# Convolution rows loaded two steps ahead, gathers placed through the step, and the second batch's convolution rearranged

## The chip, the cores and the metric

The kernel runs on one core of one Trainium2 chip. The metric is the device time of one execution in microseconds (us). The times given are the median of three runs and the profile of one further execution.

## The reference

For each of 8 batches of 4224 tokens with 192 channels the reference computes a causal convolution over 7 tokens, with one softmax-normalised set of taps for each of 8 heads of 24 channels. It then takes the real part of a two-dimensional Fourier transform over tokens and channels, adds the convolved input, normalises each token, and adds a two-layer MLP of width 768:

```python
w = softmax(weight)                                # (8, 7)
x = einsum('hk,bskhg->bshg', w, unfold(x_padded))  # causal convolution
u = x + real(fft(fft(x, axis=1), axis=2))
un = (u - mean(u)) / sqrt(var(u) + 1e-6)           # over the 192 channels
out = u + maximum(un @ w_ch1, 0) @ w_ch2
```

All matrices are used as a sum of a high and a low float16 part, so a product takes three matmuls.

## The kernel before, in words

A batch goes through these parts.

- **Convolution** (`load_windows`, L330, and `conv_unit`, L387 to L395). The tokens come in 6 chunks of 720 rows. SyncE (SP) loads a chunk as a tile `xt` of 576 KB; there are two buffers for it. TensorE (PE) multiplies it by a band matrix, three units a chunk, into PSUM tiles `pc`; ScalarE (ACT) copies these to `xa` and stores them to a scratch `sc` in DRAM (the store is issued from ACT's queue). A pass on ACT (L343) sums the squares of `xt`. For the first batch one of three copies is on VectorE (DVE, L393).
- **Fourier transform along the tokens.** SP loads `sc` back in another order as four pieces `xs` (L456, 768 to 864 KB each in four transfers, two buffers). ACT writes the high part `XH` (L472), DVE the low part `XL` (L473), in two halves a piece. Only then is the buffer free for the piece after next. `stage_a` (16 units, PE tile `pa`, L490) needs all four pieces and writes `yh` and `yl` (L498, L499). `stage_b` (8 units, `pb`, L516) writes `V` (L524, L525).
- **A step** is one of 9 tiles of a batch; eight hold 512 tokens, the last 128. `prep` makes `pq` on PE (L577), moves it to `u` on ACT (L594), adds on GpSimd (POOL) the convolved rows `xr` (L595), takes statistics on DVE (L601), works out `y` and `nm` in seven small POOL instructions (L614 to L621), normalises to `un` on ACT (L625) and splits to `hl` (ACT L635, POOL L638). `xr` is fetched by four indirect gathers a tile (`load_res`, L543), issued by POOL, into three buffers. A DMA transpose (SP, L648) turns `hl` into `kt`.
- **MLP.** Six hidden units a step (`ph` on PE, L677; `hh` on ACT, L681; `hlo` on DVE, L682) and four output units (`po`, L696 to L702; `u` on DVE, L708). `ph` has two PSUM buffers, so PE stops when ACT is two units behind. SP stores `u` (L716).

The order of the work is written in the main loop over 72 steps. In step n the MLP of tile n runs, the normalisation and transpose of tile n+2, and the sums of tile n+3. Beside these, `front` gives each batch its convolution and transform at steps counted from its own first tile (`rel`): chunk by chunk at -18 to -13, the loads of `xs` at -10 to -8, the splits at -9 to -7, `stage_a` at -7 to -5. So three batches are in work at once, and the pattern repeats every 9 steps. Each engine runs its instructions in the order that a scheduling pass makes of this. SP is one such queue: window loads, `xs` loads, transposes and stores stand in it one behind the other, and an instruction that waits holds up all behind it. A window load is moreover anchored behind the last transpose (`turn[0]`).

Ahead of the loop stand the first batch and, after its first two transposes, all six chunks of the second batch's convolution.

Of the kernel before, what the change touches and what calls it, by code (L numbers as in the profile page):

```python
# [11 lines left out]
F32 = mybir.dt.float32  # L12
I32 = mybir.dt.int32
U32 = mybir.dt.uint32
AF = mybir.ActivationFunctionType
ALU = mybir.AluOpType
# [3 lines left out]
B, S, D, HID = 8, 4224, 192, 768  # L20
# [3 lines left out]
NCH = NW // WC  # L24
# [27 lines left out]
Q0 = NPAIR  # L52
# [73 lines left out]
def kernel(  # L126
# [13 lines left out]
    nc = tc.nc  # L140
    PSUM = bass.MemoryType.PSUM
    cp = ctx.enter_context(tc.tile_pool(name="cp", bufs=1))
    sb = ctx.enter_context(tc.tile_pool(name="sb", bufs=2))
# [179 lines left out]
    def load_windows(bt, ch, tag="xt", bufs=2):  # L323

        b = bt.b
        n = D if b < NB0 else HP * GRP
        src = xw[b] if b < NB0 else xv[b - NB0]
        xt = sb.tile([WP, WC, D], F32, tag=tag, name=f"xt_{b}_{ch}", bufs=bufs)[:, :, :n]
        with tc.issue_after(turn[0]) if turn[0] else ExitStack():
            nc.sync.dma_start(xt, src[:, ch * WC : (ch + 1) * WC])  # L330
        bt.xt[ch] = xt
# [38 lines left out]
    def conv_unit(bt, ch, part, xa_slot=("xa", 2)):  # L370

        b = bt.b
        xt = bt.xt[ch]
        if part == 0:
            if ch == 0:
                scratch(bt)
            if b:
                squares(bt, xt)
            bt.xa[ch] = sb.tile(
                [WR, WC, D], F32, tag=xa_slot[0], name=f"xa_{b}_{ch}", bufs=xa_slot[1]  # L380
            )
        xa = bt.xa[ch]
        h0 = 3 * part
        n = min(3, xt.shape[2] // GRP - h0)
        pc = ps.tile([128, 3, WC, GRP], F32, tag="f", name=f"pc_{b}_{ch}_{h0}", bufs=4)
        for h in range(h0, h0 + n):
            nc.tensor.matmul(  # L387
                pc[:WR, h - h0], band[:, h, :WR], xt[:, :, h * GRP : (h + 1) * GRP],
                start=True, stop=True,
            )  # L390
        to = xa[:, :, h0 * GRP : (h0 + n) * GRP].rearrange("p w (h g) -> p h w g", g=GRP)
        if b == 0 and part == 1:
            nc.vector.tensor_copy(to, pc[:WR, :n])  # L393
        else:
            nc.scalar.activation(to, pc[:WR, :n], AF.Copy)  # L395
        if part == 2:
            cols = slice(0, xt.shape[2])
            bt.last_store = store_rows(bt, xa[:, :, cols], ch * WC * WR, cols)
            if b == 0:
                squares(bt, xt)  # L400
            del bt.xt[ch], bt.xa[ch]
# [26 lines left out]
    def scales(bt):  # L428
        bt.c = pow2_of_norm(bt.nrm, bt.nsq, 15, f"x{bt.b}")
        bt.g = sb.tile([128, 1], F32, tag="g", name=f"g_{bt.b}")  # L430
        nc.vector.reciprocal(bt.g, bt.c)
        nc.vector.tensor_scalar_mul(bt.g, bt.g, GSC)
# [8 lines left out]
    def load_x(bt, i):  # L441

        b = bt.b
        b0, b1 = PIECES[i]
        tag, bufs = (("yh", 1), ("yl", 1))[i - 2] if b == 0 and i > 1 else ("xs", 2)
        xs = sb.tile([NA, 9, D], F32, tag=tag, name=f"xs_{b}_{i}", bufs=bufs)
        for ch in range(NA // AC):

            first = 33 * AC * ch + 128 * b0 - (S if b0 >= WRAP[ch] else 0)
            src = bass.AP(  # L450
                bt.sc.tensor,
                bt.sc.offset + first * D,
                [[33 * D, AC], [128 * D, b1 - b0], [1, D]],
            )
            with tc.issue_after(turn[0]) if b == 1 else ExitStack():
                load = nc.sync.dma_start(xs[AC * ch : AC * (ch + 1), : b1 - b0], src)  # L456
        bt.xs[i] = xs
        return load.ins
# [76 lines left out]
        bt.V[it] = V  # L535


    def load_res(bt, it):
        b = bt.b
        xr = sb.tile([128, 4, D], F32, tag="xr", name=f"xr_{b}_{it}", bufs=3)  # L540
        sc = bt.sc
        def gather(g, col):
            nc.gpsimd.indirect_dma_start(  # L543
                xr[:, g], None, sc[:S],
                bass.IndirectOffsetOnAxis(ap=rows_sb[:, col : col + 1], axis=0),
            )

        for g in range(1 if it == Q0 else 4):
            gather(g, 0 if it == Q0 else 1 + 4 * it + g)
        bt.xr[it] = xr  # L550

    def prep(bt, it):
        b = bt.b
        xr = bt.xr.pop(it)
        ng = 1 if it == Q0 else 4
        pq = ps.tile([128, ND, 2, NC], F32, tag="f", name=f"pq_{b}_{it}", bufs=4)
        u = sb.tile([128, 4, D], F32, tag="u", name=f"u_{b}_{it}", bufs=5)
# [41 lines left out]
        mv = sb.tile([128, 4, 2], F32, tag="mv", name=f"mv_{b}_{it}", bufs=3)  # L599
# [8 lines left out]
        y = sb.tile([128, 4], F32, tag="y", name=f"y_{b}_{it}", bufs=3)[:, :ng]  # L608
        t = sb.tile([128, 4], F32, tag="t", name=f"t_{b}_{it}", bufs=3)[:, :ng]
        w = sb.tile([128, 4], F32, tag="w", name=f"w_{b}_{it}", bufs=3)[:, :ng]  # L610
        nm = sb.tile([128, 4], F32, tag="nm", name=f"nm_{b}_{it}", bufs=3)[:, :ng]
# [10 lines left out]
        yield  # L622
        un = sb.tile([128, 4, D], F32, tag="un", name=f"un_{b}_{it}", bufs=1)
        for g in range(ng):
            nc.scalar.activation(  # L625
                un[:, g], u[:, g], AF.Identity,
                bias=nm[:, g : g + 1], scale=y[:, g : g + 1],
            )
        yield


# [4 lines left out]
        for f, o in ((slice(0, 128), 256), (slice(128, D), D)):  # L636
            n = f.stop - f.start
# [105 lines left out]
    def call(f, *a):  # L743
        return lambda: f(*a)

    conv_at = {r: [r + 18] for r in range(-18, -12)}
    load_at = {-10: [0], -9: [1, 2], -8: [3]}
    split_at = {-9: [0, 1], -8: [2, 3, 4, 5], -7: [6, 7]}  # L750
    a_at = {-7: range(0, 4), -6: range(4, 10), -5: range(10, 16)}
    b_at = {-4: [0], -3: [1, 2], -2: [3], -1: [4], 0: [5, 6], 1: [7]}

    def front(bt, rel):
        units = []
        for ch in conv_at.get(rel, ()):
            if ch + 1 < NCH:
                units.append(call(load_windows, bt, ch + 1))
            units += [call(conv_unit, bt, ch, p) for p in range(3)]
        if rel == min(conv_at) - 1:  # L760
            units.append(call(load_windows, bt, 0))
        if bt.b > 1 and rel == max(conv_at) + 1:
            if bt.b >= NB0:
                units.append(call(conv_segments, bt))
            units.append(call(scales, bt))
        units += [call(load_x, bt, ch) for ch in load_at.get(rel, ())]
        units += [call(split_x, bt, i) for i in split_at.get(rel, ())]
        units += [call(stage_a, bt, t) for t in a_at.get(rel, ())]
        return units

    batches = [Batch(b) for b in range(B)]
# [51 lines left out]
    def sums(k):  # L823
        return [call(prep_piece, k)] * (2 if steps[k][1] == Q0 else 4)

    def rest(k):
        return [call(prep_piece, k)] * 2

# [7 lines left out]
        )  # L836
    with tc.issue_after(last_load):
        nc.sync.dma_start(rows_sb, rows)
        for ch in range(2):
            load_windows(batches[1], ch)  # L840
        for k in range(4):
            load_res(*steps[k])
    stage_b(first, 0)
    stage_b(first, 1)
    for f in sums(0) + sums(1) + rest(0):
# [2 lines left out]
    for f in rest(1):  # L848
        f()
    transposes(first, 1)  # L850
 
    for ch in range(NCH):
        for part in range(3):
            conv_unit(batches[1], ch, part)
        if ch + 2 < NCH:
            load_windows(batches[1], ch + 2)
    scales(batches[1])
    load_x(batches[1], 0)
    load_windows(batches[2], 0)
    stage_b(first, 2)  # L860
    for f in sums(2):
        f()
# [2 lines left out]
    for n in range(len(steps) + 1):  # L865
        bt, it = steps[n] if n < len(steps) else (None, 0)
        prev = steps[n - 1] if n else None
        if n + 4 < len(steps):
            load_res(*steps[n + 4])
        hid = [call(mlp_hidden, bt, it, hts) for hts in hidden_units(it)] if bt else []  # L870
        out = []
        if prev:
            out = [call(mlp_out, *prev, g) for g in range(1 if prev[1] == Q0 else 4)]
        main = []
        while hid or out:
            if hid:
                main.append(hid.pop(0))
            if out:
                main.append(out.pop(0))
        fill = []  # L880
        for f in batches:
            rel = n - f.b * NIT
            if n < len(steps) and (f.b or rel >= 0):
                fill += front(f, rel)
                fill += [call(stage_b, f, i) for i in b_at.get(rel, ())]

        at = {}

        def place(fs, first, step):
            for i, f in enumerate(fs):  # L890
                at.setdefault(min(first + i * step, len(main) - 1), []).append(f)

        if n + 2 < len(steps):
            place(rest(n + 2), 0, 1)
            place([call(transposes, *steps[n + 2])], 3, 1)
        if n + 3 < len(steps):
            place(sums(n + 3), 2, 2)
        merged = []
        for i, unit in enumerate(main):
            merged += [unit, *at.get(i, ())]  # L900
        spread(merged, fill)
# [58 lines left out]
```

## Time and profile before

| | |
|---|---|
| median of 3 runs | 1359.53 us (1359.05 to 1361.79) |
| profiled execution | 1354.9 us |
| its span, first to last instruction | 1353.0 us |
| PE busy in the span | 1193.2 us (88%) |
| ACT, DVE, POOL busy | 832.1, 738.0, 650.2 us |
| mean granted PE clock | 0.95 |

The span is the profiled execution without what lies around it (1.9 us here). A busy row of PE is time with a matmul in flight at the clock that was granted then, so a stretch at half clock counts double. A wait is the idle time of an engine ahead of an instruction, put down to what came last.

### The profile page before, as it was taken

How to read it: one execution, taken by the hardware profiler on the slowest of the kernel's cores; microseconds unless marked ns; L12 is line 12 of the kernel's file. 1: busy time of each engine (PE TensorE's matmuls, PEld its weight loads, DVE VectorE, ACT ScalarE, POOL GpSimd, SP SyncE). 2: the span in 40 equal slices, each digit the busy share in tenths (PEclk: the TensorE clock that was granted, in tenths of full speed). 3: DMA queues.
4: the chain of work that ended last, by engine and by line, in shares of the span. 5: the costliest groups of instructions: out<-in, count | busy, mean ns of one | idle time of the engine just before them, and what ended most of it. 6: DMA issues, size and time to landing. Idle time of an engine off the chain costs nothing.

```text
span 1353.0 us, 30083 instructions
## 1 busy us (share of the span) xinstructions
PE 1193.2 (88%) x12224; PEld 942.9 (70%) x12224; DVE 738.0 (55%) x1609; ACT 832.1 (62%) x1588; POOL 650.2 (48%) x1052
## 2 busy tenths in 40 slices
PE   4158679996999969999699969999889998999998
PEld 4145558785877848777587858878577775777766
DVE  7742635455655646456554555545675466555443
ACT  4655657557765757557665577656766567545642
POOL 0250455456445644447344562446654576456620
PEclk9588879998999979999799989999899999999999
DMA  8836466639554494636865376463944434223321
GB/s 269 208 99 183 120 153 174 124 98 163 147 123 108 107 183 114 129 101 106 181 144 129 104 126 166 121 124 89 213 113 111 123 89 95 71 63 86 74 62 39
DMA packets 225818, 170.18 MB, mean 126 GB/s; under 512 B 119560, under 2 KB 207440, under 8 KB 225680
## 3 DMA queue, kind: packets, MB, share of 16 engines
q1 hardware_dynamic: 163408, 108.53, 36.1%
q10 hardware_dynamic: 49600, 33.77, 9.7%
q0 software_dynamic: 12672, 25.97, 8.0%
q8 instruction: 95, 1.56, 0.5%
q14 instruction: 43, 0.35, 0.1%
HBM read 83.73 MB, written 58.55 MB: 105 GB/s over the span
## 4 chain that ended last, share of the span: by engine, by line
PE 42%; POOL 22%; issue 13%; DMA 9%; ACT 7%; DVE 5%; SPq 2%; ACTq 0%; POOLq 0%; DVEq 0%
PE ph L677 15%; POOL xr L543 10%; PE pa L490 5%; PE pc L387 5%; DMA xt<-in_xw_dram 5%; PE po L696 5%; PE po L702 4%; PE po L699 4%; POOL u L595 4%; POOL hl L638 3%; ACT un L625 2%; PE pq L577 2%; SPq L456 2%; ACT XH L472 1%; DVE XL L473 1%
## 5 line engine op out<-in xcount | busy, mean ns | idle before, releaser
L677 PE MATMUL ph<-kt,W 128*128 128x512 f16 (+1 forms) x2160 | 501.1, 365 | 44.2 <-DMA kt<-hl 29.8
L682 DVE SCALAR_TENSOR_TENSOR hlo<-ph,hh 128x512 f16<-128x512 f32 (+1 forms) x400 | 271.8, 681 | 395.2 <-ACT hh L681 394.7
L696 PE MATMUL po<-W,hh 128*128 128x192 f16 x1584 | 387.0, 247 | 7.3 <-ACT hh L681 6.3
L699 PE MATMUL po<-W,hh 128*128 128x192 f16 x1584 | 386.7, 247 | 0.0
L702 PE MATMUL po<-W,hlo 128*128 128x192 f16 x1584 | 384.1, 247 | 0.2 <-DVE hlo L682 0.2
L681 ACT ACTIVATE hh<-ph 128x512 f16<-128x512 f32 (+1 forms) x400 | 235.0, 590 | 214.8 <-PE ph L677 212.1
L543 POOL DMA_INDIRECT xr<-sc,rows_sb x264 | 276.3, 1046 | 133.3 <-issue 58.7
L677 PEld LDWEIGHTS <-W 128*128 128x128 f16 x2160 | 195.2, 99 | 190.4 <-issue 53.8
L638 POOL TENSOR_TENSOR hl<-un,hl 128x512 f16<-128x512 f32 (+1 forms) x144 | 127.8, 908 | 214.6 <-ACT hl L635 214.5
L595 POOL TENSOR_TENSOR u<-u,xr 128x768 f32<-128x768 f32 (+1 forms) x72 | 123.3, 1712 | 185.4 <-ACT u L594 185.4
L625 ACT ACTIVATE un<-u,nm,y 128x192 f32<-128x192 f32 x264 | 123.9, 537 | 86.6 <-POOL nm L621 84.4
L387 PE MATMUL pc<-xt,band 128*120 128x144 f32 x756 | 119.3, 308 | 65.4 <-DMA xt<-in_xw_dram 43.4
L696 PEld LDWEIGHTS <-hh 128*128 128x128 f16 x1584 | 155.1, 98 | 25.3 <-ACT hh L681 7.7
L702 PEld LDWEIGHTS <-hlo 128*128 128x128 f16 x1584 | 155.0, 98 | 19.7 <-issue 1.1
L699 PEld LDWEIGHTS <-hh 128*128 128x128 f16 x1584 | 155.3, 98 | 16.2 <-issue 1.3
L387 PEld LDWEIGHTS pc<-xt,band 128*120 128x120 f32 x756 | 111.0, 200 | 75.9 <-DMA xt<-in_xw_dram 45.3
L473 DVE SCALAR_TENSOR_TENSOR XL<-xs,s_x,XH 128x768 f16<-128x768 f32 x64 | 102.3, 1610 | 56.9 <-ACT XH L472 55.6
L472 ACT ACTIVATE XH<-xs,s_x 128x768 f16<-128x768 f32 x64 | 104.9, 1679 | 43.5 <-DMA xs<-sc 43.5
L490 PE MATMUL pa<-c_sb,XH 128*128 128x128 f16 x1024 | 104.8, 224 | 17.3 <-ACT XH L472 17.3
L499 DVE SCALAR_TENSOR_TENSOR yl<-pa,yh 99x512 f16<-99x512 f32 x128 | 86.4, 681 | 39.4 <-ACT yh L498 38.3
L708 DVE SCALAR_TENSOR_TENSOR u<-po,fo,u 128x384 f32<-128x384 f32 (+1 forms) x136 | 81.6, 600 | 37.4 <-PE po L702 36.7
L577 PE MATMUL pq<-c_sb,V 128*128 128x130 f16 (+1 forms) x1440 | 100.2, 215 | 1.2 <-DVE V L525 1.1
(124 smaller groups left out, 1424.3 us busy)
## 6 DMA issues: line engine op xcount, KB each, us to landing
out_dram<-u SPq DMA_DIRECT2D x64, 384.0 KB
xt<-in_xw_dram SPq DMA_DIRECT2D x42, 576.0 KB
sc<-xa ACTq DMA_DIRECT2D x42, 540.0 KB
xs<-sc SPq DMA_DIRECT2D x96, 192.0 KB
xs<-sc SPq DMA_DIRECT2D x32, 216.0 KB
xr<-sc,rows_sb POOLq DMA_INDIRECT x264
sc<-xa ACTq DMA_DIRECT2D x7, 450.0 KB
xt<-in_xv_dram SPq DMA_DIRECT2D x6, 504.0 KB
```

What stands on the lines that cost most here:

```text
L387: nc.tensor.matmul(pc[:WR, h - h0], band[:, h, :WR], xt[:, :, h * GRP : (h + 1) * GRP], start=True, stop=True,)
L490: nc.tensor.matmul(pa[:, i], x[:, at], F[:, l], start=(n == 0), stop=(n == 2))
L543: nc.gpsimd.indirect_dma_start(xr[:, g], None, sc[:S], bass.IndirectOffsetOnAxis(ap=rows_sb[:, col : col + 1], axis=0),)
L595: nc.gpsimd.tensor_tensor(u[:, :ng], u[:, :ng], xr[:, :ng], op=ALU.add)
L625: nc.scalar.activation(un[:, g], u[:, g], AF.Identity, bias=nm[:, g : g + 1], scale=y[:, g : g + 1],)
L638: nc.gpsimd.tensor_tensor(bl[:, :, o : o + n], un[:, :ng, f], hi[:, :, f], op=ALU.subtract)
L677: nc.tensor.matmul(ph[:, n], W1[:, w, ht * 128 : (ht + 1) * 128], kt[:, k], start=(i == 0), stop=(i == len(order) - 1),)
L681: anchor[0] = nc.scalar.activation(hh, ph, AF.Relu).ins
L682: nc.vector.scalar_tensor_tensor(hlo, ph, 0.0, hh, op0=ALU.max, op1=ALU.subtract)
L696: nc.tensor.matmul(po[:, g % 2], hh[:, ht, tk], W2[:, ht, 0], start=(ht == 0), stop=False)
L699: nc.tensor.matmul(po[:, g % 2], hh[:, ht, tk], W2[:, ht, 1], start=False, stop=False)
L702: nc.tensor.matmul(po[:, g % 2], hlo[:, ht, tk], W2[:, ht, 0], start=False, stop=(ht == 5),)
```

## The change

It has four parts.

1. For batches from the third on, a window load stands two chunks ahead of its convolution instead of one: chunks 0 and 1 are loaded in the two steps ahead of the first convolution, chunk c+2 behind the convolution of chunk c, whose buffer it takes. The convolutions move one step later (`rel` -17 to -12).
2. `load_res` issues one gather per call, and the calls are placed after units 1, 3, 5 and 7 of a step instead of together at its start.
3. The second batch's first four chunks are loaded at once into four tiles (two `xt` and two `xs` buffers) and convolved ahead of the loop; its last two chunks follow in step 0, its transform is loaded, split and run one or more steps later than before. All its convolution copies are on DVE.
4. The first two tiles are normalised on DVE instead of ACT.

```diff
-        if b == 0 and part == 1:
+        if b == 1 or b == 0 and part == 1:
             nc.vector.tensor_copy(to, pc[:WR, :n])
...
-    def load_res(bt, it):
+    def load_res(bt, it, g):
...
         for g in range(ng):
-            nc.scalar.activation(
-                un[:, g], u[:, g], AF.Identity,
-                bias=nm[:, g : g + 1], scale=y[:, g : g + 1],
-            )
+            if b == 0 and it < 2:
+                nc.vector.tensor_scalar(
+                    un[:, g], u[:, g], mv[:, g, 0:1], y[:, g : g + 1],
+                    op0=ALU.subtract, op1=ALU.mult,
+                )
+            else:
+                nc.scalar.activation(
+                    un[:, g], u[:, g], AF.Identity,
+                    bias=nm[:, g : g + 1], scale=y[:, g : g + 1],
+                )
...
-    conv_at = {r: [r + 18] for r in range(-18, -12)}
+    conv_at = {r: [r + 17] for r in range(-17, -11)}
...
+    conv_1 = {-9: [4, 5]}
+    load_1 = {-9: [0, 1], -8: [2, 3]}
+    split_1 = {-8: [0, 1], -7: [2, 3, 4, 5], -6: [6, 7]}
+    a_1 = {-6: range(0, 6), -5: range(6, 16)}
...
-        for ch in conv_at.get(rel, ()):
-            if ch + 1 < NCH:
-                units.append(call(load_windows, bt, ch + 1))
+        for ch in conv.get(rel, ()):
             units += [call(conv_unit, bt, ch, p) for p in range(3)]
-        if rel == min(conv_at) - 1:
-            units.append(call(load_windows, bt, 0))
-        if bt.b > 1 and rel == max(conv_at) + 1:
+            if bt.b > 1 and ch + 2 < NCH:
+                units.append(call(load_windows, bt, ch + 2))
+        if bt.b > 1 and rel in (min(conv) - 2, min(conv) - 1):
+            for ch in range(2):
+                if ch == rel - min(conv) + 2 or bt.b == 2:
+                    units.append(call(load_windows, bt, ch))
+        if rel == max(conv) + (bt.b > 1):
...
-        for ch in range(2):
-            load_windows(batches[1], ch)
-        for k in range(4):
-            load_res(*steps[k])
+        for ch in range(4):
+            load_windows(batches[1], ch, *(("xt", 2), ("xs", 2))[ch // 2])
+    for f in gathers(0) + gathers(1):
+        f()
...
     transposes(first, 1)
- 
-    for ch in range(NCH):
+    for f in gathers(2) + gathers(3):
+        f()
+    for ch in range(4):
         for part in range(3):
             conv_unit(batches[1], ch, part)
-        if ch + 2 < NCH:
-            load_windows(batches[1], ch + 2)
-    scales(batches[1])
-    load_x(batches[1], 0)
-    load_windows(batches[2], 0)
+        if ch < 2:
+            load_windows(batches[1], ch + 4)
...
-        if n + 4 < len(steps):
-            load_res(*steps[n + 4])
...
+        if n + 4 < len(steps):
+            place(gathers(n + 4), 1, 2)
```

More of the change, by code (lines that the diff above doesn't have):

```diff
@@ L535, in stage_b @@
         bt.V[it] = V
-    def load_res(bt, it):
+    def load_res(bt, it, g):
         b = bt.b
[L540 to L545, printed above, removed]
-            )
-        for g in range(1 if it == Q0 else 4):
-            gather(g, 0 if it == Q0 else 1 + 4 * it + g)
-        bt.xr[it] = xr
+        if g == 0:
+            bt.xr[it] = sb.tile([128, 4, D], F32, tag="xr", name=f"xr_{b}_{it}", bufs=3)
+        col = 0 if it == Q0 else 1 + 4 * it + g
+        nc.gpsimd.indirect_dma_start(
+            bt.xr[it][:, g], None, bt.sc[:S],
+            bass.IndirectOffsetOnAxis(ap=rows_sb[:, col : col + 1], axis=0),
+        )
     def prep(bt, it):
@@ L624, in prep @@
         for g in range(ng):
-            nc.scalar.activation(
-                un[:, g], u[:, g], AF.Identity,
-                bias=nm[:, g : g + 1], scale=y[:, g : g + 1],
-            )
+            if b == 0 and it < 2:
[7 more added lines that the diff above has]
+                    bias=nm[:, g : g + 1], scale=y[:, g : g + 1],
+                )
         yield
@@ L752 @@
     b_at = {-4: [0], -3: [1, 2], -2: [3], -1: [4], 0: [5, 6], 1: [7]}
+    conv_1 = {-9: [4, 5]}
+    load_1 = {-9: [0, 1], -8: [2, 3]}
+    split_1 = {-8: [0, 1], -7: [2, 3, 4, 5], -6: [6, 7]}
+    a_1 = {-6: range(0, 6), -5: range(6, 16)}
     def front(bt, rel):
         units = []
-        for ch in conv_at.get(rel, ()):
-            if ch + 1 < NCH:
-                units.append(call(load_windows, bt, ch + 1))
-            units += [call(conv_unit, bt, ch, p) for p in range(3)]
-        if rel == min(conv_at) - 1:
-            units.append(call(load_windows, bt, 0))
-        if bt.b > 1 and rel == max(conv_at) + 1:
+        conv, load, split, a = (
+            (conv_1, load_1, split_1, a_1) if bt.b == 1
+            else (conv_at, load_at, split_at, a_at)
+        )
+        for ch in conv.get(rel, ()):
+            units += [call(conv_unit, bt, ch, p) for p in range(3)]
+            if bt.b > 1 and ch + 2 < NCH:
[5 more added lines that the diff above has]
+        if rel == max(conv) + (bt.b > 1):
             if bt.b >= NB0:
@@ L765, in front @@
             units.append(call(scales, bt))
-        units += [call(load_x, bt, ch) for ch in load_at.get(rel, ())]
-        units += [call(split_x, bt, i) for i in split_at.get(rel, ())]
-        units += [call(stage_a, bt, t) for t in a_at.get(rel, ())]
+        units += [call(load_x, bt, ch) for ch in load.get(rel, ())]
+        units += [call(split_x, bt, i) for i in split.get(rel, ())]
+        units += [call(stage_a, bt, t) for t in a.get(rel, ())]
         return units
@@ L824, in sums, with gathers @@
         return [call(prep_piece, k)] * (2 if steps[k][1] == Q0 else 4)
+    def gathers(k):
+        bt, it = steps[k]
+        return [call(load_res, bt, it, g) for g in range(1 if it == Q0 else 4)]
     def rest(k):
```

## Prediction

> **What bounds the kernel now.** I read the page first, then PE's waits, then PE's stretches, and last the queues around one wait.
>
> ```profile
> span 1353.0 us, 30083 instructions
> PE 1193.2 (88%) x12224; PEld 942.9 (70%) x12224; DVE 738.0 (55%) x1609; ACT 832.1 (62%) x1588; POOL 650.2 (48%) x1052
> ```
>
> PE carries the time; no other engine that computes passes 62%. So the question is when PE stands still. Its waits (total, times, longest):
>
> ```profile
> PE pc L387 <- DMA xt<-in_xw_dram: 43.4, 4, 13.3
> PE ph L677 <- DMA kt<-hl: 29.8, 2, 20.9
> PE pb L516 <- ACT u L594: 7.6, 1, 7.6
> PE pc L387 <- DMA xt<-in_xv_dram: 4.1, 1, 4.1
> ```
>
> Two kinds: one wait for a window load in each of five batches (43.4 + 4.1 = 47.5 us), and waits early on. The stretches of the first batches show where the second kind lies (length, then PE busy; PEclk is the number behind POOL):
>
> ```profile
> 61.00:84.00 23.00, 21.14 (x298) 20.21 (x299) 16.25 (x25) 18.29 (x35) 12.57 (x14) 0.85 0.18 48
> 84.00:107.00 23.00, 2.07 (x16) 1.72 (x15) 3.02 (x18) 7.66 (x17) 15.01 (x27) 0.59 0.50 135
> 140.00:180.00 40.00, 21.64 (x227) 17.71 (x226) 21.87 (x48) 24.15 (x41) 26.08 (x38) 0.79 0.56 139
> 180.00:200.00 20.00, 16.83 (x136) 12.43 (x136) 10.69 (x21) 15.42 (x29) 7.14 (x13) 0.82 0.51 123
> 200.00:256.00 56.00, 56.00 (x593) 45.27 (x592) 27.69 (x60) 38.94 (x79) 28.16 (x52) 1.00 0.66 150
> ```
>
> PE idles 20.9 us in one hole (84 to 107), 18.4 + 3.2 = 21.5 us from 140 to 200, and not at all from 200 to 256. After each wait PE runs at half clock for a while; the five stretches behind the window loads, the last and their sum:
>
> ```profile
> 963.80:968.80 5.00, 5.00 (x17) 3.71 (x18) 3.91 (x5) 2.82 (x5) 4.48 (x8) 0.50 1.02 186
> sum 21.30, PE 21.30 PEld 19.61 DVE 15.59 ACT 16.65 POOL 4.48; mean PE 4.26 PEld 3.92 DVE 3.12 ACT 3.33 POOL 0.90
> ```
>
> Half of 21.3 us is lost: 10.65. The Trainium skill, TensorE: Matmul & The Clock Gate, Part 1, says the full clock returns after about 3.4 us of sustained work, which would make it 5 x 3.4 / 2 = 8.5 us; the rows here run to 5.0 us, and I keep them.
>
> The queue around one such wait, on SP, and what stood still for it on ACT and PE:
>
> ```profile
> 468.10 6.23 SPq L648 DMA_TRANSPOSE kt<-hl  x1
> 474.42 5.83 SPq L456 DMA_DIRECT2D xs<-sc  x4
> 480.30 0.68 SPq L330 DMA_DIRECT2D xt<-in_xw_dram  x1
> ```
> ```profile
> 492.21 3.10 ACT L472 ACTIVATE XH<-xs,s_x 128x768 f16<-128x768 f32 x2 [9.44 <-DMA xs<-sc]
> 494.29 3.91 PE L387 MATMUL pc<-xt,band 128*120 128x144 f32 x16 [13.28 <-DMA xt<-in_xw_dram]
> ```
>
> The window load is issued at 480.3, when PE is already at its convolution. Note the second stall: ACT waits 9.4 us for `xs` at the same time.
>
> **Part 1, the windows two steps ahead.** SP's order at this place before and after, a number behind a tile's name being its chunk, piece or step (the last number is a serial):
>
> ```order
> 107 L648 DMA_TRANSPOSE kt_2_5940<-hl_2_5884 128x12x128
> 108 L456 DMA xs_2_5925<-sc_3644 32x8x192 x4
> 109 L330 DMA xt_1_5958<-in_xw_dram 128x1152
> 110 L456 DMA xs_3_6090<-sc_3644 32x8x192 x4
> 111 L648 DMA_TRANSPOSE kt_3_6150<-hl_3_6086 128x12x128
> ```
> ```order
> 107 L651 DMA_TRANSPOSE kt_2_5930<-hl_2_5847 128x12x128
> 108 L330 DMA xt_1_5992<-in_xw_dram 128x1152
> 109 L456 DMA xs_2_5941<-sc_3843 32x8x192 x4
> 110 L456 DMA xs_3_6066<-sc_3843 32x8x192 x4
> 111 L719 DMA out_dram<-u_0_5131 128x768
> 112 L651 DMA_TRANSPOSE kt_3_6124<-hl_3_6060 128x12x128
> ```
>
> `xt_1` now goes ahead of `xs_2`, and its convolution stands more than a step later. The 47.5 us and the 10.65 us of slow clock go. What is late next is `xs_2`. ACT, before and after (`hh_1` is step 1's hidden unit, `xa_0` the copy of chunk 0):
>
> ```order
> 500 L472 ACTIVATE XH<-xs_1_5896,s_x_5332 128x64x12 x2
> 501 L635 ACTIVATE hl_3_6086<-un_3_6030 128x4x192
> 502 L613 ACTIVATE sd_4_6239<-mv_4_6163,eps 128x4
> 503 L681 ACTIVATE hh_1_6020<-ph_1_2_6152 128x512
> 504 L472 ACTIVATE XH<-xs_2_5925,s_x_5332 128x64x12 x2
> ```
> ```order
> 476 L355 DMA sc_6175<-xa_0_6179 120x6x192 x2
> 477 L684 ACTIVATE hh_1_5994<-ph_1_1_6071 128x512
> 478 L472 ACTIVATE XH<-xs_1_5925,s_x_5555 128x64x12 x2
> 479 L610 ACTIVATE sd_4_6229<-mv_4_6140,eps 128x4
> 480 L684 ACTIVATE hh_1_5994<-ph_1_2_6129 128x512
> 481 L472 ACTIVATE XH<-xs_2_5941,s_x_5555 128x64x12 x2
> ```
>
> The split of `xs_2` stays behind the same hidden unit, but the store of chunk 0 has come between. How long does `xs_2` take undisturbed? The last batch shows it, having no convolution beside it:
>
> ```profile
> 1111.00 1.81 SPq L456 DMA_DIRECT2D xs<-sc  x4
> 1111.00:1116.00 5.00, 4.84 (x44) 3.51 (x42) 3.92 (x14) 3.10 (x6) 4.43 (x6) 1.00 0.82 173
> 1116.00:1118.00 2.00, 2.00 (x24) 1.41 (x21) 2.00 (x4) 1.60 (x2) 1.76 (x1) 1.00 0.22 58
> ```
>
> About 5 us at 173 GB/s. With chunk 0's 540 KB beside its 768 KB the same rate gives 7.6 us. The piece can be asked for only when DVE has done its half of `xs_0`, which the groups put some 1.9 us behind ACT's (1.6 for most, more for the wider one). ACT's own instructions in between are three copies, three `hh`, two splits and a small one:
>
> ```profile
> L395 ACT ACTIVATE xa<-pc 120x432 f32<-120x432 f32 (+1 forms) x138 | 62.2, 478 | 18.5 <-PE pc L387 13.5 <-issue 1.2 <-DMA sc<-xa 1.2
> L681 ACT ACTIVATE hh<-ph 128x512 f16<-128x512 f32 (+1 forms) x400 | 235.0, 590 | 214.8 <-PE ph L677 212.1 <-PE pa L490 1.2 <-DVE hlo L682 0.7
> L472 ACT ACTIVATE XH<-xs,s_x 128x768 f16<-128x768 f32 x64 | 104.9, 1679 | 43.5 <-DMA xs<-sc 43.5
> L473 DVE SCALAR_TENSOR_TENSOR XL<-xs,s_x,XH 128x768 f16<-128x768 f32 x64 | 102.3, 1610 | 56.9 <-ACT XH L472 55.6 <-DMA xs<-sc 0.8
> ```
>
> That is 3 x 0.48 + 3 x 0.59 + 2 x 1.68 + 0.3 = 6.8 us. I take a new wait of 7.6 + 1.9 - 6.8 = 2.7 us a batch, 13.5 us in all, between none (PE's own pace leaves ACT later) and 9.4 us (as now). Does 2.7 us cost clock? Two short waits and what followed:
>
> ```profile
> 1014.60 1.24 PE L677 MATMUL ph<-kt,W 128*128 128x512 f16 x5 [2.13 <-DVE hlo L682]
> 1014.60:1019.60 5.00, 5.00 (x56) 3.82 (x56) 3.10 (x5) 3.36 (x8) 1.79 (x2) 1.00 0.67 138
> 1124.57 0.26 PE L696 MATMUL po<-W,hh 128*128 128x192 f16 x1 [3.63 <-ACT hh L681]
> 1124.50:1129.50 5.00, 4.56 (x20) 2.10 (x21) 3.54 (x4) 5.00 (x8) 2.38 (x2) 0.66 0.10 16
> ```
>
> 2.13 us left the clock full, 3.63 us did not; two `ph` buffers hide part of ACT's wait from PE, so I charge nothing. Part 1: 47.5 + 10.65 - 13.5 = 44.7 us gained.
>
> **Part 2, the gathers**, at nothing: in the order they still stand four in a row behind POOL's add, since each needs a buffer that this add frees. The hole shows the same, below.
>
> **Parts 3 and 4, the first two batches.** What ends the hole at 107 is `kt` of step 0, and that hangs on POOL, which issues eight gathers (first and last) ahead of the small instructions:
>
> ```profile
> 85.86 0.99 POOL L543 DMA_INDIRECT xr<-sc,rows_sb  x1 [0.15 <-POOL u L595]
> ...
> 96.17 0.22 POOL L617 TENSOR_TENSOR t<-y 128x4 f32<-128x4 f32 x1
> ```
>
> In the new order POOL has not moved away from that:
>
> ```order
> 13 L592 TENSOR_TENSOR u_1_775<-u_1_775,xr_1_653 128x768
> 14 L544 DMA xr_3_849<-sc_126,rows_sb 128x192 x4
> 15 L544 DMA xr_4_1177<-sc_126,rows_sb 128x192 x4
> 16 L611 TENSOR_SCALAR w_0_763<-mv_0_751 128x4
> 17 L612 TENSOR_SCALAR nm_0_764<-mv_0_751 128x4
> ```
>
> So the hole ends where it did, and normalising on DVE (eight instructions) buys at most a microsecond; nothing. But the hole is filled: PE's order now has there the convolution of chunks 2 and 3, five units of `stage_b` and one `pq`, which ACT's order confirms (`V_3` and `u_2` ahead of step 0's `hl_0`, where before `un_0` stood directly ahead of it). Prices: a chunk (x16), a unit (x24), a `pq` (x18):
>
> ```profile
> 461.76 2.12 PE L387 MATMUL pc<-xt,band 128*120 128x144 f32 x16
> 129.50:130.80 1.30, 1.26 (x24) 1.11 (x24) 1.00 0.87 312
> 459.66 1.19 PE L577 MATMUL pq<-c_sb,V 128*128 128x130 f16 x18
> ```
>
> 2 x 2.12 + 5 x 1.26 + 1.19 = 11.7 us taken out of later stretches. From 140 to 200 the two large waits go: 7.6 us (PE behind ACT, which sat on `xs`) and 29.8 - 20.9 = 8.9 us (`kt` of step 2, which is now made before step 0 is done). The row for ACT's wait there:
>
> ```profile
> 142.35 6.55 ACT L472 ACTIVATE XH<-xs,s_x 128x768 f16<-128x768 f32 x4 [6.38 <-DMA xs<-sc]
> ```
>
> `xs` still follows its last store at the same distance, so I leave 6 us of the 21.5 standing (bounds: none and all) and gain 15.5. Half clock in the first batches costs 18.2 / 2 = 9.1 us now (first and sum of four windows); the first stays, another may: gain 4.6.
>
> ```profile
> 107.00:112.00 5.00, 5.00 (x15) 2.13 (x14) 0.87 (x2) 1.19 (x2) 0.50 (x1) 0.50 0.73 151
> sum 18.20, PE 18.16 PEld 11.19 DVE 6.09 ACT 9.89 POOL 10.56; mean PE 4.54 PEld 2.80 DVE 1.52 ACT 2.47 POOL 2.64
> ```
>
> Against it: ACT's squares of chunks 2 and 3 now stand between the first `yh` copies, 2 x (1.15 + 0.20) = 2.7 us, and DVE's `yl` follow them; all on the path. The 12 DVE copies at 0.59 us lie in the hole, where DVE works 3.02 of 23 us.
>
> ```profile
> L343 ACT ACTIVATE sq<-xt 128x1152 bf16<-128x1152 f32 (+1 forms) x48 | 55.2, 1150 | 22.3 <-DMA xt<-in_xw_dram 22.1 <-ACT xa L395 0.2
> L393 DVE COPY xa<-pc 120x432 f32<-120x432 f32 x6 | 3.6, 592 | 0.0
> ```
>
> Sum: 11.7 + 15.5 + 4.6 - 2.7 = 29.1 us.
>
> **Total.** 44.7 + 29.1 = 73.8 us. The profiled execution took 1354.9 us (1353.0 and 1.9 around it), the median of the runs is 1359.5, 0.3% above; its distance I keep: 1359.5 - 73.8 = 1285.7 us. Its own range, 1272 to 1300, is the new wait between 0 and 5 us a batch and a few us early on.
>
> **Rivals.**
> - *The `xs` wait takes the place of the window wait.* For: ACT's 9.4 us end only 2 us before PE's 13.3. By the Trainium skill, DMA: Bandwidth & Descriptors, "Issuing engines are not separate DMA queues", all transfers share the same 16 engines and interleave, so a load issued earlier only pushes another one back. Against: the 5 us above. Then 5 x 9.4 = 47 us come back with their slow clock, part 1 gives 0.5, and the time is 1359.5 - 29.1 - 0.5 = 1330. Chance 0.16; that the window itself still lands late is in it.
> - *The first batches gain nothing*, because ACT and POOL pass their delay on: 1359.5 - 44.7 = 1315. Chance 0.11.
> - *Everything goes*: no new wait, and all 21.5 and 6.6 of clock early: 1359.5 - 58.2 - 11.7 - 21.5 - 6.6 = 1262. Chance 0.09.
> - *Slower.* A window load must now wait for a convolution and a square of its own step, and the transposes `kt_5` to `kt_7` stand behind it in SP's queue. One that lands after its step began costs like step 2's, 8.9 us. There are three a batch in six batches: 18 x 8.9 = 160, 1446 us; it decides from nine late ones (73.8 / 8.9 = 8.3). Against: a transpose has over a step of slack. Chance 0.04.
> - *No change that shows* (within 0.2%, about what a measurement can tell here): 0.02.
>
> **How the numbers follow.** The forecast has 0.58. The range 1260 to 1330 takes in the first three rivals and leaves out little else. Faster 0.58 + 0.16 + 0.11 + 0.09 = 0.94, same 0.02, slower 0.04.
>
> **What would show it.** Right: no `pc` wait on `xt` from the third batch on, an ACT wait for `xs` under 5 us a batch, PE over 10 us busier between 84 and 107, the first `ph` still near 107, POOL's gathers still four in a row. Wrong: ACT's waits on `xs` as long as now with PE idle beside them, or PE waits on `kt`.

## The result and the profile after

The changed kernel takes 1314.4 us (median of four runs, 1311.8 to 1317.4) against 1359.3 for the kernel before: ratio 0.9675, 95% interval 0.9638 to 0.9712. A second set of five runs gave 1313.9 us and 0.9707 (0.9686 to 0.9727). So 39 to 45 us went, where the prediction had 73.8.

The profiled execution took 1317.4 us, its span is 1315.6:

```profile
span 1315.6 us, 30115 instructions
PE 1194.7 (91%) x12224; PEld 942.4 (72%) x12224; DVE 746.8 (57%) x1635; ACT 821.3 (62%) x1562; POOL 645.0 (49%) x1052
```

PE works as long as before (1193.2 us) and idles 120.9 us instead of 159.8. PE's waits (total, times, longest):

```profile
PE po L699 <- ACT hh L684: 36.8, 15, 7.4
...
PE po L699 <- DVE u L711: 7.0, 4, 4.3
PE ph L680 <- DMA kt<-hl: 5.7, 1, 5.7
...
PE pc L387 <- DMA xt<-in_xw_dram: 0.3, 1, 0.3
```

The window waits (47.5 us) are gone. In their place PE waits in `po`, mostly for ACT's `hh`: once in each of the same five batches, 7.39, 7.40, 6.40, 6.03 and 4.31 us, 31.5 in all. The first batches, in the stretches that the prediction showed of before (length, PE busy; PEclk is the third number from the end):

```profile
61.00:84.00 23.00, 19.04 (x272) 17.99 (x273) 17.35 (x26) 19.55 (x35) 11.72 (x13) 0.82 0.25 77
84.00:107.00 23.00, 18.20 (x167) 17.30 (x164) 12.41 (x39) 5.81 (x15) 15.00 (x27) 0.70 0.58 168
107.00:140.00 33.00, 26.97 (x244) 19.59 (x243) 17.44 (x52) 18.78 (x40) 21.70 (x35) 0.90 0.72 182
140.00:180.00 40.00, 34.03 (x284) 24.86 (x283) 25.24 (x42) 31.44 (x48) 18.88 (x27) 0.96 0.85 206
180.00:200.00 20.00, 20.00 (x244) 17.00 (x242) 12.62 (x28) 15.96 (x33) 9.90 (x15) 1.00 0.49 120
```

The stretch from 107 to 140 in the kernel before:

```profile
107.00:140.00 33.00, 32.00 (x271) 23.80 (x270) 9.28 (x20) 17.36 (x35) 0.77 (x2) 0.92 0.70 205
```

PE does 16.1 us more in the hole and 15.6 more from 140 to 200, but 2.1 less before and 5.0 less from 107 to 140. The first `ph` of step 9, where the second batch's MLP begins, comes at 271.9 instead of 295.1 us: 23.2 us of the span's 37.4 come from the first batches, 14.2 from everything behind.

The slow clock behind the five waits did not go either; the last of five stretches, and their sum:

```profile
928.40:933.00 4.60, 4.56 (x20) 2.58 (x20) 2.76 (x3) 4.60 (x11) 0.73 (x1) 0.50 0.57 190
sum 23.30, PE 23.26 PEld 15.24 DVE 8.18 ACT 19.11 POOL 8.46; mean PE 4.65 PEld 3.05 DVE 1.64 ACT 3.82 POOL 1.69
```

Half of 23.3 us is lost, 11.7, where it was 10.65. One of the stalls on SP, on ACT and on PE:

```profile
605.39 9.52 SPq L456 DMA_DIRECT2D xs<-sc  x8
```
```profile
605.10 0.90 ACTq L355 DMA_DIRECT2D sc<-xa  x2
...
616.42 3.09 ACT L472 ACTIVATE XH<-xs,s_x 128x768 f16<-128x768 f32 x2 [6.01 <-DMA xs<-sc]
```
```profile
621.80 0.34 PE L699 MATMUL po<-W,hh 128*128 128x192 f16 x1 [6.40 <-ACT hh L684]
```

ACT waits 6.0 us for piece 2 of `xs`, which lands 11.0 us after it was asked for; chunk 0's store went out 0.3 us ahead of it. That store is larger than the prediction and the expectation of experiment 2 have it: `x2` in its row are two transfers of 540 KB each, since `store_rows` writes the first rows of a batch a second time behind the end of `sc`. By the trace's DMA packets 1080 KB went out on ACT's queue from 605.9 to 612.2 us. The profile's page counts six such transfers for each of seven batches, where five chunks are of that size:

```profile
sc<-xa ACTq DMA_DIRECT2D x42, 540.0 KB
```

Behind the split of piece 2 stand `un` and the next `hh`, for which PE waits. In the five batches ACT's wait is 7.0, 7.0, 6.0, 5.7 and 5.8 us. So the theory was: the store (with the gathers) stretches the load. Against it: the load is asked for too late; or ACT has something else to wait for.

### The profile page after: what moved, and what is told of

Same layout as the page of the kernel before. It is cut to its first block, busy times and chain, and to the rows that moved or that the text cites. A ratio compares the mean times of both kernels' runs of the same rounds, so it can differ in the third digit from the quotient of the medians.

```text
span 1315.6 us, 30115 instructions
## 1 busy us (share of the span) xinstructions
PE 1194.7 (91%) x12224; PEld 942.4 (72%) x12224; DVE 746.8 (57%) x1635; ACT 821.3 (62%) x1562; POOL 645.0 (49%) x1052
## 4 chain that ended last, share of the span: by engine, by line
PE 38%; POOL 18%; issue 14%; ACT 11%; DMA 8%; DVE 5%; SPq 2%; ACTq 0%; POOLq 0%; DVEq 0%
PE ph L680 14%; POOL xr L544 8%; DMA xs<-sc 6%; PE po L699 4%; PE po L705 4%; PE po L702 4%; PE pa L490 4%; POOL u L592 4%; ACT XH L472 3%; PE pq L574 3%; POOL hl L641 3%; ACT un L628 2%; PE pc L387 2%; DVE XL L473 2%; PE pb L516 2%
## 5 line engine op out<-in xcount | busy, mean ns | idle before, releaser
L544 POOL DMA_INDIRECT xr<-sc,rows_sb x264 | 268.3, 1016 | 136.5 <-issue 59.4
L628 ACT ACTIVATE un<-u,nm,y 128x192 f32<-128x192 f32 x256 | 120.0, 537 | 73.1 <-POOL nm L618 72.7
L387 PE MATMUL pc<-xt,band 128*120 128x144 f32 x756 | 118.9, 297 | 21.8 <-DMA band<-line_d 14.7
L387 PEld LDWEIGHTS pc<-xt,band 128*120 128x120 f32 x756 | 105.6, 190 | 29.5 <-issue 14.7
L490 PEld LDWEIGHTS <-XH 128*128 128x128 f16 x1024 | 82.3, 99 | 28.1 <-ACT XH L472 18.0
```

Source lines behind the costliest of these rows:

```text
L387: nc.tensor.matmul(pc[:WR, h - h0], band[:, h, :WR], xt[:, :, h * GRP : (h + 1) * GRP], start=True, stop=True,)
L490: nc.tensor.matmul(pa[:, i], x[:, at], F[:, l], start=(n == 0), stop=(n == 2))
L544: nc.gpsimd.indirect_dma_start(bt.xr[it][:, g], None, bt.sc[:S], bass.IndirectOffsetOnAxis(ap=rows_sb[:, col : col + 1], axis=0),)
L628: nc.scalar.activation(un[:, g], u[:, g], AF.Identity, bias=nm[:, g : g + 1], scale=y[:, g : g + 1],)
```

## The experiments

The runs were made in three sets, each with its own runs of the kernel before (medians 1356.3, 1353.0 and 1351.9 us), so ratios are compared. Experiments 1, 2, 6 and the first run of 8 are of the first set, 4 and 5 of the second, 3, 7 and the second run of 8 of the third.

**1. A third `xs` buffer**, so that piece 2 is asked for with pieces 0 and 1.

```
-        ... else ("xs", 2)
+        ... else ("xs", 3)
```

> The changed kernel with three xs buffers in place of two, so that the load of piece 2 is asked for together with pieces 0 and 1 instead of waiting until VectorE has finished with piece 0. Theory (the load is late, by its asking or by its rate): ScalarE's waits on xs from the third batch on fall from some 7 us to under 2 us a batch, the five waits of po (31.5 us) to under 8 us in all, and most of the 11.7 us that half clock costs behind them goes: 1314.4 falls to about 1278 (1270 to 1288). Rival (ScalarE has more to do in that step than fits, and the load only stands in front of it): the waits of po on hh stay above 3 us a batch with no wait on xs ahead of them, and the time falls by under 15 us, to 1300 or more.

Measured: 1311.8 us, 0.9669 (0.9642 to 0.9695): no gain that shows. The load now comes in time, and the rival came nearer, though not with ACT's own work. On ACT, POOL and PE at the same place:

```profile
611.37 1.86 ACT L628 ACTIVATE un<-u,nm,y 128x192 f32<-128x192 f32 x4 [4.28 <-POOL nm L618]
```
```profile
601.18 0.19 POOL L614 TENSOR_TENSOR t<-y 128x4 f32<-128x4 f32 x1
601.53 1.06 POOL L544 DMA_INDIRECT xr<-sc,rows_sb  x1 [0.16 <-POOL t L614]
...
606.32 1.18 POOL L544 DMA_INDIRECT xr<-sc,rows_sb  x1 [0.30 <-issue]
607.52 1.33 POOL L615 TENSOR_TENSOR t<-t,w 128x4 f32<-128x4 f32 x1
```
```profile
613.76 0.34 PE L699 MATMUL po<-W,hh 128*128 128x192 f16 x1 [4.72 <-ACT hh L684]
```

The wait for `xs` gone, ACT waits 4.3 us for `nm`, and the reason stands on POOL: four gathers have gone in between two small operations of one normalisation (`t`, 601.18 and 607.52). The same four stood there in the changed kernel, but `nm` was ready 1.0 us before ACT's split began. Here the small operations behind the gathers are slow as well, 1.33 and 1.35 us instead of 0.21 and 0.19, and DVE's split of piece 2, early now, stands beside them:

```profile
607.29 2.98 DVE L473 SCALAR_TENSOR_TENSOR XL<-xs,s_x,XH 128x768 f16<-128x768 f32 x2
```

PE's five waits fall only from 31.5 to 23.9 us. A second thing was late by a little less, and the edit itself seems to have made it later.

**2. The store one step later** in the program (`held[0]` issues chunk 0's store).

```
+            if bt.b > 1 and ch == 1:
+                units.append(lambda: held[0]())
             units += [call(conv_unit, bt, ch, p) for p in range(3)]
```

> The changed kernel with the store of chunk 0 (540 KB) issued one step later, at the head of chunk 1, from the third batch on; nothing else is moved. Theory that the store's bytes beside the load stretch it: piece 2 (768 KB) lands in some 7 to 8 us instead of 12, ScalarE's wait for it falls from 7 to 2 to 3 us, the five waits of po from 31.5 to some 10 us, and the time to about 1290 (1282 to 1298). Rival, that the load is asked for too late whatever lies beside it: the wait stays at 6 us or more and the time within 5 us of 1314.

Measured: 1311.5 us, 0.9651 (0.9617 to 0.9686), ACT's wait 6.0 us. It told nothing, since the store had not moved; ACT's queue and SP's:

```profile
601.07 2.04 ACTq L355 DMA_DIRECT2D sc<-xa  x2
...
613.46 3.09 ACT L477 ACTIVATE XH<-xs,s_x 128x768 f16<-128x768 f32 x2 [5.99 <-DMA xs<-sc]
```
```profile
601.37 9.51 SPq L461 DMA_DIRECT2D xs<-sc  x8
```

Written a step later, the store was ready as early as ever, and the scheduler put it back.

**3. The store held for certain**, on ACT's queue behind a copy of chunk 1.

```
+            if b > 1 and ch == 1 and part == 1:
+                with tc.issue_after(copy.ins):
+                    held[0]()
```

> The changed kernel with the store of chunk 0 held on ScalarE's queue behind the second copy of chunk 1, from the third batch on (in the run named e2 the store had still been issued at its old place, 0.3 us ahead of the load, so that one told nothing). Theory that the store's bytes stretch the load beside them: piece 2 lands 7 to 8 us after it is asked for instead of 12, and ScalarE's wait for it falls from 6 to 7 us to under 3; GpSimd's nm behind four gathers is then the later one, as with the third buffer, so the five waits of po fall only to some 24 us and the time stays within 6 us of 1314. Rival (the load is only asked for too late, or the gathers alone stretch it): the wait for xs stays above 5 us.

SP, then ACT:

```profile
606.32 9.84 SPq L464 DMA_DIRECT2D xs<-sc  x8
```
```profile
612.37 3.49 ACT L480 ACTIVATE XH<-xs,s_x 128x768 f16<-128x768 f32 x2 [1.02 <-DMA xs<-sc]
619.01 1.86 ACT L636 ACTIVATE un<-u,nm,y 128x192 f32<-128x192 f32 x4 [3.15 <-POOL nm L626]
...
642.91 3.93 ACTq L355 DMA_DIRECT2D sc<-xa  x2
646.89 0.60 ACT L692 ACTIVATE hh<-ph 128x512 f16<-128x512 f32 x1 [4.01 <-issue]
```

The load lands 6.05 us after it is asked for instead of 11.0, and ACT waits 1.0 us instead of 6.0 (0.9 to 1.3 in the five batches). The gathers kept their place on POOL's queue, so it was the store (in the changed kernel the load, once late, also meets the gathers of 607.9 to 613.9 us). By the Trainium skill, DMA: Bandwidth & Descriptors, "Issuing engines are not separate DMA queues", transfers of all queues interleave on the same 16 engines; the two runs agree with it, 11.0 us with the store beside the load and 6.05 without, at 278 and 187 GB/s for the whole core from 607 to 612 us. `nm` is then the later one, as expected. The time is 1320.0 us, 0.9773 (0.9742 to 0.9804), worse than the changed kernel: the stores of chunks 0 and 1 now go out together, ACT stands some 4 us in their issue, four times in the run, and PE waits 2.5 to 3.0 us for `hh` behind each.

**4. The changed kernel again, part 2 taken back, and the gathers held.** The first two were to show what the written order of the gathers does; the third puts each tile's gathers, on POOL's queue, behind the normalisation of the tile three steps earlier, the one that frees their buffer:

```
-        G_.tensor_tensor(nm, nm, y, op=ALU.mult)
+        normed[b * NIT + it] = G_.tensor_tensor(nm, nm, y, op=ALU.mult).ins
...
+        last = normed.get(b * NIT + it - 3)
+        with tc.issue_after(last) if last else ExitStack():
+            nc.gpsimd.indirect_dma_start(
```

> The changed kernel itself once more, beside the three below on the same chip, since the kernels of the first four runs lie within a few us of one another: 1314 (1310 to 1318).

> The changed kernel with part 2 taken back: a step's four gathers are again written at its start instead of two units apart. By the prediction part 2 does nothing, since four gathers stand in a row behind GpSimd's addition in either order: within 3 us of the changed kernel. Rival (the written order does reach the queue): over 5 us more.

> The changed kernel with the gathers of every step held on GpSimd's queue behind the normalisation (y, nm) of the tile three steps earlier, so that no four gathers stand between its small operations. Two xs buffers as in the changed kernel. Theory (two things are late by nearly as much, ScalarE's load of piece 2 and GpSimd's nm behind four gathers, and the later one sets the time): the load still ends at the same place, the five waits of po stay at 25 to 31 us, and the time stays within 5 us of the changed kernel. Rival (GpSimd's queue alone is what holds ScalarE): the waits fall to under 10 us and the time to about 1285.

Measured: the changed kernel 1313.9 us (0.9707, 0.9686 to 0.9727), part 2 taken back 1315.5 (0.9721, 0.9700 to 0.9743): no difference that shows. The gathers held: **1297.5 us**, 0.9588 (0.9568 to 0.9608), 16.4 us under the changed kernel. So the theory for this run failed (the load was to stay late and the time within 5 us), and the rival is closer, though it had 1285 and under 10 us of waits: five of 2 us and four of 1.8 remain, 17.0 in all. Of the 14.7 us between this trace and that of the changed kernel in the same set, 1.8 lie ahead of step 9, 12.9 behind. SP, POOL, ACT and PE of that run, one stall's place:

```profile
589.88 9.71 SPq L456 DMA_DIRECT2D xs<-sc  x8
```
```profile
593.45 0.20 POOL L622 TENSOR_TENSOR nm<-nm,y 128x4 f32<-128x4 f32 x1
593.80 2.09 POOL L548 DMA_INDIRECT xr<-sc,rows_sb  x1
```
```profile
593.68 1.86 ACT L632 ACTIVATE un<-u,nm,y 128x192 f32<-128x192 f32 x4
595.45 0.57 ACT L688 ACTIVATE hh<-ph 128x512 f16<-128x512 f32 x1
595.93 3.39 ACT L472 ACTIVATE XH<-xs,s_x 128x768 f16<-128x768 f32 x2
...
602.99 0.90 ACTq L355 DMA_DIRECT2D sc<-xa  x2
```
```profile
608.72 0.26 PE L703 MATMUL po<-W,hh 128*128 128x192 f16 x1 [1.95 <-ACT hh L688]
```

With `nm` early, `un` stands ahead of the split of piece 2, the split finds its load landed (595.93, at most 6.05 us after asking), and chunk 0's store goes out 13 us behind the load instead of beside it. One edit on POOL's queue removed both late things, because the scheduler then puts chunk 0 and its store elsewhere. The clock stays full directly behind four of the five waits of 2 us, but not behind the four of 1.8 us, 8 us later in the same batches. One batch, both stretches:

```profile
608.70:613.70 5.00, 4.76 (x43) 3.59 (x44) 2.53 (x3) 5.00 (x7) 4.37 (x5) 1.00 1.00 153
617.10:622.10 5.00, 4.09 (x41) 3.87 (x41) 4.62 (x11) 1.63 (x4) 1.46 (x7) 0.66 0.57 137
```

So each of the five batches still has one stretch of 3.4 us at half clock, up to 8.5 us lost in all where the changed kernel lost 11.7.

**5. Both edits**, the third buffer and the gathers held.

> Both edits together: the third xs buffer and the gathers behind the normalisation. Theory of two waits side by side, neither of which gives anything alone: the five waits of po fall from 31.5 us to under 10 us in all and most of the half clock behind them (11.7 us) goes, so about 1285 (1277 to 1297). Rival (a third wait just as late, or the edits trade places with something in the first two batches): the waits stay above 15 us and the time above 1300.

Measured: 1302.3 us, 0.9619 (0.9600 to 0.9638). Better than the changed kernel, but not than the gathers alone: with the store out of the way two buffers do. So the theory (1285) fell: PE's waits in `po` stay at 20.2 us in the five batches, 5.4 of them one wait for `hh` in the last.

**6. Part 1 alone**: the kernel before with the windows of the third batch and later two steps ahead.

```
-    conv_at = {r: [r + 18] for r in range(-18, -12)}
+    conv_at = {r: [r + 17] for r in range(-17, -11)}
...
+            if ch + 2 < NCH:
+                units.append(call(load_windows, bt, ch + 2))
```

> The kernel before with the windows of the third batch and later loaded two steps ahead, and nothing else of the change (the first two batches and the gathers as before). By the prediction's own sum for this part, 44.7 us, it would take 1359.3 - 44.7 = 1315. By the profile after, where the waits of 47.5 us on the windows came back as 31.5 us on hh behind the load of xs, with about as much half clock as before: 16 us, so about 1343 (1338 to 1348).

Measured: 1336.1 us, 0.9845 (0.9819 to 0.9872): 20.2 us, near the 16 read from the profile after and under half of 44.7. PE's five waits here are 4.9 us each, all on `hh`, and ACT at one of them waits for POOL:

```profile
632.56 1.86 ACT L625 ACTIVATE un<-u,nm,y 128x192 f32<-128x192 f32 x4 [4.77 <-POOL nm L621]
```

So with part 1 alone it is `nm` and not the load that is late. The rest of the change (parts 3 and 4) is the difference to the whole: 0.9845 - 0.9707 to 0.9845 - 0.9675, or 19 to 23 us.

**7. The gathers held in the kernel before, without and with part 1.**

> The kernel before with nothing but the gathers held behind the normalisation three tiles earlier. Theory: in the kernel before the wait of PE on the windows (47.5 us) stands ahead of the one on nm and covers it; the waits on xt stay above 40 us and the time falls by under 10 us (a few us at most from the first two batches). Rival (the gathers cost the same 16 us wherever they stand): 16 us or more.

> The kernel before with the windows two steps ahead and the gathers behind the normalisation. Theory: part 1 gave 20 us instead of the 44.7 of the prediction because nm was late by nearly as much as the windows; with nm early it gives 35 to 45 us against the run named e10: about 1308 (1300 to 1315). Rival (the two edits add, 20 and what e10 gives): 1325 or more.

Measured: without part 1, 1319.2 us, 0.9761 (0.9732 to 0.9789); with part 1, 1331.3 us, 0.9843 (0.9811 to 0.9874). Both theories fell (the first run's rival, 16 us or more, came), and so did what the prediction began with. PE's wait for the windows is gone from the kernel before, although they are still asked for one step ahead; its waits, and SP at the place that the prediction showed:

```profile
PE ph L681 <- DMA kt<-hl: 26.4, 2, 18.2
PE ph L681 <- DVE hlo L686: 25.2, 28, 3.0
...
PE pc L387 <- DMA xt<-in_xw_dram: 0.6, 1, 0.6
```
```profile
449.33 1.44 SPq L652 DMA_TRANSPOSE kt<-hl  x1
450.82 0.90 SPq L330 DMA_DIRECT2D xt<-in_xw_dram  x1
456.31 4.48 SPq L456 DMA_DIRECT2D xs<-sc  x4
```

In the kernel before, SP had here `kt_2` (its issue alone 6.23 us), `xs_2`, then `xt_1`. With the gathers held, `kt_2` is issued in 1.44 us, ahead of chunk 0's store (454.5) and not beside it, and the scheduler puts `xt_1` ahead of `xs_2`. Which of the two made the window come in time was not separated; either way a lead of two steps was not needed. Of the 38.0 us between the two traces, 7.9 lie ahead of step 9. With part 1 on top the collision only moves: at the longest of PE's waits (6.9 us) the output's store, from which a `u` buffer comes free, runs beside chunk 0's; SP and ACT:

```profile
629.99 0.40 SPq L720 DMA_DIRECT2D out_dram<-u  x1
```
```profile
629.93 0.36 ACTq L355 DMA_DIRECT2D sc<-xa  x1
...
639.31 1.21 ACT L598 ACTIVATE u<-pq,g 128x384 f32<-128x384 f32 x3 [7.08 <-DMA out_dram<-u]
```

**8. The hole at the start**: the gathers of steps 3 and 4 behind `hl_0` and `hl_1` of the first batch, in the changed kernel and with all gathers held (`tail` is the last operation of `hl`).

```
+        if b == 0:
+            behind[it + 3] = tail.ins
...
+        with tc.issue_after(behind[it]) if late else ExitStack():
+            nc.gpsimd.indirect_dma_start(
```

> The changed kernel with the gathers of steps 3 and 4 held on GpSimd's queue behind the low halves hl_0 and hl_1 of the first batch; the gathers of later steps as they were. Theory (the end of the hole is set by GpSimd's queue, where eight gathers, 88 to 98 us, stand ahead of the small operations of the normalisation): the first ph starts near 105 instead of 115 us and the time falls by 8 us, to about 1306. Rival (the eight gathers only move, and u_3 and kt_3 come late instead): the first ph comes near 105, but PE waits as much more between 110 and 160 us, and the time stays within 3 us of 1314.

> The gathers behind the normalisation as in the run named e6 (1297.5), and those of steps 3 and 4 further back, behind hl_0 and hl_1 of the first batch as in e3. Theory (the first ph starts near 102 us as in e3, and what follows keeps it): about 1291. Rival (in the first batches something else comes late by as much, the windows of the second batch or kt): within 3 us of 1297.

The first `ph` in the changed kernel and in the first of these:

```profile
114.97 4.43 PE L680 MATMUL ph<-kt,W 128*128 128x512 f16 x10 [5.70 <-DMA kt<-hl]
```
```profile
103.86 2.32 PE L686 MATMUL ph<-kt,W 128*128 128x512 f16 x10 [1.97 <-DMA kt<-hl]
...
143.16 3.90 PE L686 MATMUL ph<-kt,W 128*128 128x512 f16 x10 [4.28 <-DMA kt<-hl]
```

The hole does end 11 us earlier (7.6 against the changed kernel's second profile), 2.3 of them because `stage_a` began earlier in that run. But the time is 1312.8 us, 0.9677 (0.9649 to 0.9705): no gain that shows. A wait of 4.3 us for `kt` and one of 2.7 us for a window come later instead, so the rival held. With all gathers held the first `ph` is at 102.0 us already (no extra edit), and the extra edit gives 1296.1 us, 0.9589 (0.9550 to 0.9629), no different from 1297.5.

## Why the prediction was partly right

**The direction and the rivals.** Faster was right, and the time lies in the range, 28.7 us over the forecast. It lies between the forecast and the rival in which the `xs` wait takes the window wait's place (1330): that mechanism is what happened, at 31.5 of the 47.5 us. The rival in which the first batches gain nothing has almost the measured number (1315), but by chance, as the first batches gained 23.2 us.

**The step that failed is in part 1: "I take a new wait of 7.6 + 1.9 - 6.8 = 2.7 us a batch", and "so I charge nothing" for the clock.** ACT's wait was 5.7 to 7.0 us, PE's 4.3 to 7.4, and 11.7 us of slow clock came back. Three things were wrong in it:
- The 7.6 us. The load took 11.0 us beside the store, and 6.05 with the store held. The prediction counted 540 KB for the store, though its own order line has `x2` behind `120x6x192`: 1080 KB. Its sum with both transfers, (768 + 1080) / 173 = 10.7 us and 10.7 + 1.9 - 6.8 = 5.8 us a batch, would have met ACT's wait. That it comes so near is partly luck: the core moved 278 GB/s and not 173 from 607 to 612 us, of which by the DMA packets the store had 185, the load 80 and the gathers 11.
- The hiding. "Two `ph` buffers hide part of ACT's wait from PE" did not hold: PE stood in `po`, which needs `hh`, and in four of the five batches it waited longer than ACT (6.40 and 6.01 us in the rows above). In the prediction's own rows a wait of 3.63 us was already followed by a slow clock.
- What was late next was looked for in one place only. Behind `xs_2` stood POOL's `nm`, late by 4.3 to 4.8 us once the load was in time (2.9 to 3.2 with the store held). The prediction saw the four gathers in a row (part 2) and saw in the hole that they stand ahead of the small operations, but charged that to the first batch alone and not to the five later ones.

The 13.5 us of the sum became 31.5 + 11.7 = 43.2 in the trace, and these 29.7 us are most of what was missing. Part 1 alone gave 20.2 us for 44.7.

**A premise that failed.** The prediction took the window wait as a matter of how early the window is asked for. The gathers held in the kernel before removed it with the old lead. Its own lines had a sign: the transpose ahead of the window on SP took 6.23 us to issue, where 1.4 us is its length elsewhere.

**Part 2** at nothing was right for the change as made: in a row in either order, 1.6 us between the two, inside the intervals. That the gathers cost nothing did not follow: holding them is worth 16 us on the changed kernel and 33 on the kernel before.

**Parts 3 and 4**: 29.1 us predicted, 19 to 23 measured by difference. The traces have 23.2 and 26.5 us up to step 9, of which part 1 alone gives 1.9. Term by term: the hole filled 16.1 us for 11.7; the stalls from 140 to 200 gave 15.6 for 15.5; the squares cost less than the 2.7, as `stage_a` and its copies took 0.8 us longer up to the first `pb`; most of the 2.1 us that PE does less before 84 is that `stage_a` began 1.6 us later. What was missing is that the hole's end moved: the first `ph` came at 114.97 (111.4 in the second profile) and not "near 107", 5.0 us of PE's time from 107 to 140. The last term, 4.6 us of clock, was not measured apart.

Of "what would show it", the windows, the hole's filling and the gathers came as written; the wait for `xs` (5.7 to 7.0, not under 5) and the first `ph` did not.

## What to carry to other kernels

When a large store and the loads of the same step share the DMA engines, the one that is waited for first decides: find which transfer stands beside the store in the trace, count every transfer that the store makes (here two of 540 KB and not one), and price the load by a row in which it really stood beside one. A wait that is removed shows the next one, so look on every engine that feeds the waiting one (here POOL's small operations behind its own DMA issues) before booking the gain; here two waits of nearly the same length gave nothing one at a time. Under a scheduler an edit can act by moving something else (here the store), and an edit in the written order may move nothing, so read the order of the queues before reading the time.

## What the runs showed of the hardware

- A load of 768 KB, asked for in four parts, had landed 6.05 us after the first was asked for, and 11.0 us with a store of 1080 KB (two transfers of 540 KB) beside it. A transpose beside such a store held SP's queue 6.23 us instead of 1.44, and a store beside other stores held ACT's 3.93 instead of 0.90.
- With the gathers held, waits of 1.94 to 2.12 us left the clock full behind them in four of five cases, but behind the four waits of 1.76 to 1.78 us it fell to half for 3.4 us: the length of the wait alone did not decide. After waits of 4.3 to 7.4 us, in the changed kernel, it stayed at half for 3.2 to 6.0 us of PE's work.
- Some POOL operations of 0.2 us took 1.3 us and more, and some gathers 2 us instead of 0.95. The slow ones stand beside DVE's splits `XL`: with the third buffer, 14 of the 16 small operations of the normalisation that overlap one took over 1 us, and none of the 432 others; with the gathers held, 25 of 30 gathers that overlap one took over 1.3 us, and 1 of the 234 others. No run moved the splits alone, so the cause is not shown.
